# New orders of the instructions on all five queues of a pre-norm attention and GLU block

## The chip, the cores and the metric

One core of one Trainium2 chip runs the kernel. The metric is device time in microseconds (us) of one execution; a comparison is one of medians of such times. Below, PE is the matrix engine, DVE the vector engine, ACT the activation engine, POOL the general engine, and SP a queue that only issues transfers (DMAs); ACT issues a few too.

## The reference

Two blocks on 2048 tokens of width 448: linear attention with 16 heads of 28, then a gated feed-forward layer of width 1792, each behind a layernorm and with a residual.

```python
def _A_ref(x, wqkv, wo):
    qkv = (x @ wqkv).reshape(B, S, 3, H, Dh) ...
    phi = lambda t: jnp.where(t > 0, t + 1, jnp.exp(t)) + 1e-6
    pq, pk = phi(q), phi(k)
    kv = jnp.einsum("bhsd,bhse->bhde", pk, v)
    z = jnp.einsum("bhsd->bhd", pk)
    num = jnp.einsum("bhqd,bhde->bhqe", pq, kv)
    den = jnp.einsum("bhqd,bhd->bhq", pq, z)[..., None] + 1e-6
    return (num / den) ... @ wo
def _B_ref(x, w_gate, w_up, w_down):
    return (_gelu(x @ w_gate) * (x @ w_up)) @ w_down
h = x + _A_ref(_layernorm(x), A_wqkv, A_wo)
h2 = h + _B_ref(_layernorm(h), B_w_gate, B_w_up, B_w_down)
```

## The kernel before

The tokens are 16 tiles of 128 (numbers 0 to 15). V is never formed: the kernel sums phi(k) with the normalised input over all tokens, applies the V weights once, folds in wo, and gets the attention output from phi(q) normalised by its denominator.

**A graph and an order written out.** Every operation is a numbered task with a name; `_Graph.add` records what it reads and writes and from that its dependencies. `ORDERS` holds five strings, for PE, ACT, DVE, POOL and SP: the numbers of the tasks in the order in which each engine executes them. `place` takes them as they are, `plan` works out which semaphores each task waits for (a wait that another wait implies is dropped), and `emit` writes the instructions. An engine takes its tasks strictly in that order, so a task whose wait is not over holds back all that stand behind it. `HOLD` says which of several waits of a task is issued first.

**Stage 1, first layernorm and K, Q.** For tile t: `bnst1_t` and `bnag1_t` (DVE, lines 440 and 441) give the statistics, `ln1_t` and `rstd1_t` (ACT, 447 and 449) the reciprocal deviation, `negm1_t` (POOL, 444) minus the mean, and `normD_t` (DVE) or `normP_t`, `normT_t` (POOL, 507 and 510) the normalised tile. From tile 8 on, ln and rstd take two tiles at once. Tiles 0 to 3 are transposed on PE (`tr_t`) and copied out by `evxA_t` and `evxD_t`; the later ones by DMA transposes on SP (`xT_4` to `xT_14`, line 514; from tile 8 on two tiles each). `K2K3a`, `K2K3b` and so on are the projections of two tiles, in two halves, `K0`, `Q0`, `K1`, `Q1` those of one (536, 555). `ekN_t`, `ckN_t`, `pkN_t` (ACT, DVE, DVE; N tiles from t) make phi(k); `eqN_t` and `rqN_t` (ACT, 598 and 599) start phi(q). `pt10_t`, `pt30_t` and their like (PE, 590) are the sums over tokens.

**Stage 2.** `evp...`, `z0`, `z1` copy the sums out; `kv`, `kvm`, `w2a`, `w2b`, `evwA_g`, `evwD_g` form the product of the sums with the V and output weights, and eight small DMAs `dw2_0` to `dw2_7` repack it. For each pair of tiles p: `cq`, `aq` (DVE), `t1p` (POOL, 682), `dr`, `deA`, `rd`, `pn` (DVE, ACT) normalise phi(q); `pd` is a small copy on POOL; `oT_p` transposes by DMA (719); `outa_p`, `outb_p` are the output projection (751) and `hr` adds the residual. Pair 0 goes over PE transposes and copies (`tro`, `evoA`, `evoD`, `out1`). Then the second layernorm: `bnst2`, `bnag2`, `ln2`, `rstd2` (tiles 0 and 1) or `vpe2`, `pow2` (POOL, later tiles), `nhD` or `nhP`, `wrap`, and the transposes `trh` (PE, tiles 0 and 1) or `hT_t` (DMA, 807).

**Stage 3, feed-forward.** `guN_v` is block v of gate and up matmuls for N tiles (874 and 876, alternating between the two halves of the PE rows); `ge` is the gelu on ACT (898), `hm` the product on DVE (900). Tiles go in chunks of 2, 2, 4, 4 and 4: blocks 0 to 6, 7 to 13, 14 to 27, 28 to 41 and 42 to 55. `downa_t`, `downb_t` are the down projection of tiles t and t + 1 (825), `fo896_t` adds the residual (830) and `do_t` writes the output (814, 832). The last two tiles go one by one (843, 847). Gate and up of blocks share the PSUM banks 0, 1, 6 and 7, the down and the output projections 2, 3 and 4, 5.

**Transfers.** SP loads x, the K and Q weights, then issues the transposes, `dwv`, `dwv_t`, `dwo`, `dwg0` (gate weights) and `dwd_0` to `dwd_3` (down weights); ACT issues `dwu0` (up weights). All plain loads of a queue are chained in the order of their making:

```python
def dma(q, out_ap, in_ap, w, name, r=(), behind=()):
    own = [t for t in behind if t.eng == q]
    far = [t for t in behind if t.eng != q]
    t_ = G.add(q, lambda e: e.dma_start(out_ap, in_ap), r=r, w=w, name=name, kind="dma", after=own + last[q], sync=far)
    last[q] = [t_]
```

`after` only binds the order on the same queue; `sync` is a wait.

Of the kernel before, what the change touches and what calls it, by code (L numbers as in the profile page):

```python
# [12 lines left out]


ORDERS = (
# [29 lines left out]
)  # L45
HOLD = {
# [11 lines left out]
}  # L58

# [169 lines left out]
def bass_sequential_preLN__linear_attn_block__glu_gated_geglu__prompt_kernel(  # L229
    nc, A_x, A_wqkv, A_wo, B_x, B_w_gate, B_w_up, B_w_down, out  # L230
):
    S, D, FF, H, DH = 2048, 448, 1792, 16, 28
# [14 lines left out]
    WVQ = "sp"  # L247
# [14 lines left out]
    with es:  # L262
        block = es.enter_context(nc.Block())

        def sb(name, shape, dt):
            return es.enter_context(nc.sbuf_tensor(name, shape, dt))
# [6 lines left out]
        wv_sb = sb("wv_sb", [128, 4, D], BF16)  # L273
# [43 lines left out]
        def bufs(name, n):  # L317
            return [_Buf("%s%d" % (name, i)) for i in range(n)]
# [5 lines left out]
        b_w, b_wv = {"Q": bufs("wq", 3), "K": bufs("wk", 3)}, bufs("wv", 2)  # L324
# [18 lines left out]
        A_, B_ = slice(0, 64), slice(64, 128)  # L343
# [19 lines left out]
            return t_  # L363
# [4 lines left out]
        def rows3(src, c0, c1):  # L368
            return src[0:384, c0:c1].rearrange("(k p) n -> p k n", p=128)
# [240 lines left out]
            proj2(what)  # L610

        xts = [t for t in G.all if t.name.startswith("xT_")]
        dma(WVQ, wv_sb[:, 0:3, :], rows3(A_wqkv, 2 * D, 3 * D), [b_wv[0]], "dwv", behind=xts[3:4])
        dma(WVQ, wv_sb[A_, 3, :], A_wqkv[384:448, 2 * D:3 * D], [b_wv[1]], "dwv_t", behind=xts[3:4])
        dma(WVQ, wo_sb[:, :, :], A_wo.rearrange("(g p) n -> p g n", p=GW), [b_wo], "dwo", behind=xts[3:4])
        dma("sp", wgu_sb[A_, :, :], B_w_gate.rearrange("(k p) n -> p k n", p=64), b_wg, "dwg0", behind=xts[-1:])
        dma("act", wgu_sb[B_, :, :], B_w_up.rearrange("(k p) n -> p k n", p=64), b_wu, "dwu0", behind=xts[-1:])
# [355 lines left out]
```

## Time and profile before

| | before |
|---|---|
| three runs | 193.38, 193.20, 192.89 us, median 193.20 |
| the profiled execution | 193.26 us, its span 191.3 us |
| granted PE clock | 1.000 |
| busy in the span | PE 184.7, weight loads 101.3, DVE 125.3, ACT 71.4, POOL 52.4 us |
| DMA | 17.59 MB, mean 92 GB/s |

The span goes from the first to the last instruction that the profile shows; the execution is 2.0 us longer. Busy time is that of an engine's instructions, without waits; ends of matmuls are modelled, so PE looks a little busier than it is. A row of the timeline has the start from the span's beginning, the length, the engine and line, what is written and read, the shapes, and in brackets the idle time before it with what ended it. The chain that ended last is the sequence of work and waits that leads back from the last instruction.

### The profile page before, as it was taken

What the parts mean: (1) busy time and instruction counts of PE and PEld (TensorE: products, weight loads), DVE (VectorE), ACT (ScalarE), POOL (GpSimd) and SP (SyncE); (2) the same over time, 40 slices, a digit from 0 to 9 for tenths busy, and PEclk for the clock granted to TensorE, in tenths of its full rate; (3) what the DMA queues carried; (4) which work ended last, traced back from release to release, by engine and by line L of the source; (5) the groups of instructions that cost most, each with busy time, mean ns of one, the idle gap of its engine ahead of it and who ended that gap; (6) DMA issues with size and microseconds to landing.
All of it is one profiled execution on the core that took longest, in us unless ns stands there. A gap on an engine that the chain in (4) does not pass through costs nothing.

```text
span 191.3 us, 4741 instructions
## 1 busy us (share of the span) xinstructions
PE 184.7 (97%) x2010; PEld 101.3 (53%) x2010; DVE 125.3 (65%) x260; ACT 71.4 (37%) x164; POOL 52.4 (27%) x102
## 2 busy tenths in 40 slices
PE   7999899999799999999999999999999999999995
PEld 7544355554587667864444444454444444455443
DVE  2999748899999989996576837453444233444304
ACT  3686333699773203222223231232422213144100
POOL 5268910253045476701314420610000000000000
DMA  5933679995279623393302091000039000130002
GB/s 174 335 97 82 116 118 245 259 279 108 76 160 220 143 48 58 70 162 66 58 2 55 3 171 25 0 0 3 0 88 155 0 0 3 71 121 3 0 0 99
DMA packets 34244, 17.59 MB, mean 92 GB/s; under 512 B 27312, under 2 KB 32944, under 8 KB 34224
## 3 DMA queue, kind: packets, MB, share of 16 engines
q1 hardware_dynamic: 33472, 15.34, 36.8%
q10 hardware_dynamic: 752, 1.95, 3.8%
q8 instruction: 16, 0.26, 0.6%
q14 instruction: 4, 0.03, 0.1%
HBM read 8.37 MB, written 1.84 MB: 53 GB/s over the span
## 4 chain that ended last, share of the span: by engine, by line
PE 75%; DMA 11%; DVE 9%; SPq 2%; issue 0%; ACT 0%; POOL 0%
PE ps L874 30%; PE ps L825 18%; PE ps L876 7%; PE ps L555 6%; PE ps L590 4%; PE ps L751 4%; DVE st L440 3%; DMA hnT<-hn 3%; DMA pqnT<-pqn 3%; DMA x_sb<-in_A_x_dram 3%; PE ps L843 3%; DMA hh<-xnn 2%; SPq L361 1%; PE ps L736 1%; DVE pk L575 1%; SPq L807 1%
## 5 line engine op out<-in xcount | busy, mean ns | idle before, releaser
L874 PE MATMUL ps<-hnT,wgu_sb 64*128 64x512 bf16 (+1 forms) x490 | 88.7, 333 | 0.4 <-DMA hnT<-hn 0.4
L876 PE MATMUL ps<-hnT,wgu_sb 64*128 64x512 bf16 (+1 forms) x490 | 88.6, 333 | 0.0
L898 ACT ACTIVATE gl<-ps 128x256 bf16<-128x256 f32 (+1 forms) x84 | 35.0, 453 | 87.9 <-PE ps L874 86.7
L900 DVE TENSOR_TENSOR hh<-ps,gl 128x256 bf16<-128x256 f32 (+1 forms) x84 | 40.2, 507 | 38.4 <-ACT gl L898 38.1
L874 PEld LDWEIGHTS ps<-hnT,wgu_sb 64*128 64x128 bf16 x490 | 45.8, 94 | 34.1 <-DMA hnT<-hn 1.2
L876 PEld LDWEIGHTS ps<-hnT,wgu_sb 64*128 64x128 bf16 x490 | 45.8, 94 | 2.7
L825 PE MATMUL ps<-wd_sb,hh 64*128 64x448 bf16 x392 | 39.4, 349 | 0.0
L825 PEld LDWEIGHTS ps<-wd_sb,hh 64*128 64x128 bf16 x392 | 19.0, 94 | 18.6 <-issue 0.4
L555 PE MATMUL ps<-wqk_sb,hh 64*128 64x448 bf16 x196 | 23.4, 350 | 0.5 <-DMA hh<-xnn 0.3
L682 POOL TENSOR_TENSOR t<-pq,zbc 128x448 f32<-128x448 bf16 x15 | 16.0, 1084 | 24.9 <-DVE zbc L619 12.5
L440 DVE BATCH_NORM_STATS2 st<-x_sb 128x6 f32<-128x448 bf16 x32 | 19.1, 612 | 3.6 <-DMA x_sb<-in_A_x_dram 3.3
L830 DVE TENSOR_TENSOR x_sb<-ps,x_sb 128x896 bf16<-128x896 f32 x7 | 7.6, 1090 | 12.8 <-PE ps L825 12.8
L590 PE MATMUL ps<-pk,xnn 64*128 64x448 bf16 x128 | 15.2, 350 | 0.5 <-DVE pk L575 0.4
L555 PEld LDWEIGHTS ps<-wqk_sb,hh 64*128 64x128 bf16 x196 | 9.0, 94 | 10.4 <-PE ps L555 1.5
L572 ACT ACTIVATE e<-ps 128x896 bf16<-128x896 f32 (+1 forms) x10 | 7.5, 760 | 7.4 <-PE ps L555 7.4
L751 PE MATMUL ps<-w2p,pqnT 64*128 64x448 bf16 x84 | 9.9, 349 | 0.4 <-DMA pqnT<-pqn 0.4
L774 POOL TENSOR_SCALAR hn<-x_sb,nm,rs 128x448 bf16<-128x448 bf16 x14 | 9.9, 714 | 0.4
L590 PEld LDWEIGHTS ps<-pk,xnn 64*128 64x128 bf16 x128 | 6.1, 94 | 7.2 <-DVE pk L575 2.0
L686 DVE TENSOR_REDUCE den<-t 128x32 f32<-128x896 f32 (+1 forms) x9 | 8.8, 973 | 1.7 <-POOL t L682 1.6
L575 DVE SCALAR_TENSOR_TENSOR pk<-ps,e 128x896 bf16<-128x896 f32 (+1 forms) x10 | 9.0, 904 | 0.2
L758 DVE TENSOR_TENSOR x_sb<-ps,x_sb 128x896 bf16<-128x896 f32 (+1 forms) x9 | 8.8, 978 | 0.1
L507 POOL TENSOR_SCALAR xnn<-x_sb,nm,rs 128x448 bf16<-128x448 bf16 (+1 forms) x12 | 8.3, 695 | 2.0 <-ACT rs L449 1.7
(85 smaller groups left out, 138.4 us busy)
## 6 DMA issues: line engine op xcount, KB each, us to landing
wgu_sb<-in_B_w_gate_dram SPq DMA_DIRECT2D x1, 1568.0 KB, 14.6
wgu_sb<-in_B_w_up_dram ACTq DMA_DIRECT2D x1, 1568.0 KB, 16.5
out_dram<-x_sb SPq DMA_DIRECT2D x7, 224.0 KB, 2.3
x_sb<-in_A_x_dram SPq DMA_DIRECT2D x3, 448.0 KB, 6.1
wd_sb<-in_B_w_down_dram SPq DMA_DIRECT2D x2, 448.0 KB, 5.0
wqk_sb<-in_A_wqkv_dram SPq DMA_DIRECT2D x2, 336.0 KB, 4.9
wd_sb<-in_B_w_down_dram SPq DMA_DIRECT2D x2, 336.0 KB, 6.3
wo_sb<-in_A_wo_dram SPq DMA_DIRECT2D x1, 392.0 KB, 5.9
```

The costliest lines, as they stand in the source:

```text
L440: op("dve", lambda e: e.bn_stats(st[:, t, :], src_ap), [b_src], [b_st[t]], "bnst%s_%d" % (tag, t))
L555: ins = e.matmul(ps[:, bk0 + i_, 0:D], xnT[HALF[h], t, c, :], wqk_sb[HALF[h], c, c0:c0 + D], start=(part == "a" and c == 0), stop=(c == 3))
L575: op("dve", lambda e: e.scalar_tensor_tensor(pk[:, ip:ip + n, :], psK, EPS, e1[:, i:i + n, :], ALU.max, ALU.add), b_ps[bu:bu + n] + b_e1[i ...
L590: ins = e.matmul(ps[:, BK_PT[c], 0:D], xnn[HALF[h], t // 2, tcols(t, c)], pk[HALF[h], t % PK_R, :], start=(t == 0 and o == 0), stop=(t == ...
L682: op(eng, lambda e, t=t, n=n: e.tensor_tensor(t1[:, n, :], pq[:, t, :], zbc[:, :], ALU.mult), [b_pq[t]] + b_z, [b_t1[n]], "t1%s_%d" % (eng ...
L751: ins = e.matmul(ps[:, BK_OUT[n], 0:D], pqnT[rows, i2, n, g, :], w[rows, g, :], start=(g == 0 and s == 0), stop=(g == 3 and s == 1))
L774: op("pool", lambda e, t=t, sh=sh: e.tensor_scalar(hn[:, sh, 0:D], x_sb[:, t, :], nm2[:, t:t + 1], rs2[:, t:t + 1], ALU.add, ALU.mult), [b ...
L825: ins = e.matmul(ps[:, BK_O[n], 0:D], hh[HALF[h], j, (t % HR) * 128:(t % HR + 1) * 128], wd_sb[HALF[h], j, :], start=(s == 0 and j == 0), ...
L874: first = e.matmul(psG[:, jj * N:(jj + 1) * N], wgu_sb[A_, k, j * 128:(j + 1) * 128], hnT[A_, r0:r0 + nt, ka_, :], start=(k == 0), stop=(k ...
L876: ins = e.matmul(psU[:, jj * N:(jj + 1) * N], wgu_sb[B_, k, j * 128:(j + 1) * 128], hnT[B_, r0:r0 + nt, kb_, :], start=(k == 0), stop=(k = ...
L898: G.add("act", lambda e, gi=gi, cs_=cs_, psG=psG: e.activation(gl[:, gi, cs_], psG[:, cs_], AF.Gelu_apprx_tanh), r=[b_ps[BK_G[i]]], w=b_gl ...
L900: op("dve", lambda e, dst=dst, srcU=srcU, srcL=srcL: e.tensor_tensor(dst, srcU, srcL, ALU.mult), [b_ps[bu]] + b_glh, [b_ar[j_][t % HR] for ...
```

## The change

The five orders are new, and with them `HOLD`. The same tasks are executed, none is added or removed. In the last hunk the loads of the V weights no longer name the fourth transpose as something that they stand behind.

What moves, by name:

- SP: `xT_7` before `xT_6`; `dw2_0` to `dw2_3` before `oT_1`; `dwd_1` to `dwd_3` before `oT_2`; `oT_7` before `oT_6`; `hT_8` before `hT_10`; `do_0` from before `oT_5` to behind `hT_10`; `do_4` before `hT_14`; `do_6` from before `hT_14` to behind `do_12`, near the end; `do_12` and `do_6` before `do_14`.
- ACT: `evxA_0` before `ln1_1`; `ln1_4` and `rstd1_4` before `evxA_3` and `eq1_1`; `ln1_7` and `rstd1_7` before `ln1_6`; `dwu0` behind `ek1_15` and `ek1_14`; `rq2_4` before `z1`; `evwA_0` before `deA2_2` and `evoA_0`; `eq2_10` before `evoA_1`; many exchanges of neighbours.
- DVE: `bnag1_1` behind `evxD_0`; `bnst1_5` before `evxD_3`; the statistics of tiles 14 and 15 behind `pk2_4`; `ptpad` and `wvpad` to the front; `aq_4` before `evpD_3`; `cq_6` before `evwD_1`; `pn1_1` and `pn2_2` later; `aq_10`, `dr2_14`, `wrap2_8`, `wrap2_10` earlier; `fo896_2` 14 places later, `fo896_6` 14 earlier and `fo896_10` 14 later; many exchanges.
- POOL: `eps` before `ones`; `mones`, `mask_a`, `mask_b` to the front; `mhalf` and `powwarm` from the front to between the `t1p`; `normP_7`, `normT_7` before `normP_6`; `t1p_10` before `nhP_3`; `pd_14` before `vpe2_8` and `pd_12`.
- PE: `K1` before `Q1`; `pt30_4` and several other sums behind the next projection; `Q10Q11a` before `w2a`; `outa_5`, `outb_5` three places earlier, `downb_2` six later; even blocks before odd ones through most of chunks 2 and 3; `downa_6` two and `downb_6` six places earlier; `downa_10` two and `downb_10` five later.

The diff, cut where `HOLD` and the context are long (task numbers used here: 255, 256 `dwv`; 323, 361 `oT_1`, `oT_2`; 324 to 331 `dw2_0` to `dw2_7`; 332 to 335 `dwd_0` to `dwd_3`; 571, 595 `hT_12`, `hT_14`; 424, 543, 547 `do_0`, `do_4`, `do_6`; 98, 99 `ln1_4`, `rstd1_4`; 259 `dwu0`):

```diff
@@ -13,47 +13,46 @@
 
 
 ORDERS = (
-    "27 33 757 61 41 65 49 80 58 68 83 84 72 76 77 92 78 73 79 93 74 90 111 112 75 88 91 135 89 136 118 116 155 119"
-    " 117 156 140 175 142 141 176 143 160 195 162 196 161 215 180 216 181 163 182 231 200 232 201 223 183 224 202 225"
-    " 226 203 227 228 235 229 230 236 239 266 240 269 268 243 270 271 244 247 288 248 291 294 295 251 252 311 307 336"
-    " 400 337 403 406 409 412 362 418 415 363 421 386 422 449 387 452 455 435 458 461 436 464 467 470 498 501 471 507"
-    " 504 484 513 510 485 519 516 558 525 559 522 531 582 528 583 537 534 540 601 596 541 606 611 616 544 621 626 631"
-    " 636 641 545 651 646 661 656 666 679 674 667 689 684 670 699 671 694 709 704 719 714 729 724 739 734 744 748 745"
+    "27 33 757 61 41 65 49 68 58 80 83 84 76 72 77 92 73 93 78 79 74 75 111 88 112 90 89 135 91 136 118 155 116 156"
+    " 117 119 175 140 176 142 141 195 143 160 196 162 161 215 163 216 180 231 181 232 200 182 201 183 223 224 202 225"
+    " 226 203 227 228 235 229 230 236 239 266 240 243 268 269 270 271 244 247 288 248 291 294 295 251 252 311 307 336"
+    " 400 337 403 406 409 412 362 418 415 363 421 386 422 449 387 452 455 435 458 461 436 464 467 470 498 501 484 504"
+    " 507 485 510 513 471 516 519 558 522 525 559 528 531 582 534 537 583 540 596 601 541 611 544 606 545 616 621 626"
+    " 631 636 641 646 651 656 661 666 674 679 667 689 684 699 694 670 709 704 719 714 671 729 724 739 734 744 748 745"
     " 751 754",
-    "1 3 26 30 31 38 39 34 46 54 47 62 42 55 66 50 67 81 59 98 99 69 105 82 106 122 85 129 123 130 148 149 95 94 168"
-    " 169 113 188 208 189 209 137 157 177 197 259 220 217 233 260 263 234 264 237 281 285 238 241 242 320 274 245 289"
-    " 272 292 246 249 250 304 305 302 303 312 308 254 357 253 314 401 404 407 381 413 410 419 416 430 450 453 479 456"
-    " 459 462 465 468 553 499 502 508 577 505 514 511 520 517 526 523 532 529 538 535 602 604 597 599 607 609 614 612"
-    " 619 617 622 624 629 627 632 634 637 639 644 642 654 652 647 649 662 664 659 657 680 682 677 675 690 687 685 692"
-    " 702 700 697 695 712 710 707 705 722 720 717 715 732 730 727 725 740 742 737 735",
-    "28 29 36 32 37 44 35 52 45 40 53 25 48 43 63 64 96 51 97 60 127 103 128 104 120 70 121 71 144 146 86 147 87 145"
-    " 206 166 164 207 165 186 167 187 184 185 204 114 205 115 138 139 158 159 178 179 315 198 199 316 221 222 218 276"
-    " 219 277 24 352 262 261 278 280 265 284 282 286 267 283 319 287 273 275 321 290 322 293 353 296 297 300 301 298"
-    " 299 310 306 376 313 474 309 356 377 358 359 338 425 339 402 380 426 341 405 408 340 382 342 383 411 414 429 420"
-    " 347 417 364 350 365 548 475 572 367 366 431 368 432 423 478 451 549 388 454 389 457 391 392 390 374 480 460 552"
-    " 463 398 437 466 481 469 440 573 438 554 500 439 555 503 441 576 509 472 506 578 515 579 512 486 487 521 488 489"
-    " 490 518 527 560 447 524 563 561 564 496 533 562 530 539 536 584 587 585 586 603 605 600 588 598 542 608 610 613"
-    " 594 618 615 570 620 623 625 630 628 633 635 638 640 645 643 546 655 653 648 650 663 665 660 658 683 678 676 681"
-    " 668 688 691 686 693 703 701 672 698 696 713 711 708 706 723 721 718 716 733 731 728 726 741 743 738 736 746 749"
+    "1 3 26 30 31 34 38 46 39 47 62 42 54 55 66 50 67 98 99 59 69 105 106 129 81 82 130 85 122 148 123 149 94 95 168"
+    " 169 113 188 189 137 208 209 157 177 197 220 217 259 233 234 260 263 264 281 237 285 238 242 241 274 272 320 289"
+    " 245 292 246 250 249 304 305 302 303 312 308 254 357 253 314 401 404 407 381 410 413 419 430 416 450 453 456 459"
+    " 479 553 462 465 468 577 499 502 505 508 511 514 517 520 523 526 529 532 535 538 599 597 604 602 614 607 612 609"
+    " 617 619 622 624 627 629 634 632 637 639 644 642 649 647 652 654 657 659 662 664 675 677 682 680 692 690 687 685"
+    " 700 695 702 697 712 710 705 707 722 720 717 715 732 730 725 727 740 742 735 737",
+    "25 28 29 36 32 44 35 45 37 52 40 48 53 24 63 43 64 96 51 97 103 60 104 127 70 128 144 71 120 145 146 121 147 86"
+    " 87 164 166 167 165 184 186 187 185 114 115 206 204 207 205 138 139 158 159 315 178 179 276 198 199 277 218 219"
+    " 316 221 222 352 353 262 261 278 280 265 284 286 282 267 283 319 376 273 275 287 290 321 293 322 296 297 300 301"
+    " 298 299 310 474 306 313 377 309 356 425 358 359 475 338 402 341 426 380 342 339 405 408 382 383 340 411 414 429"
+    " 420 431 347 417 364 350 367 548 365 368 549 366 432 478 423 451 388 389 454 391 572 392 390 374 457 552 460 398"
+    " 573 463 480 437 466 481 469 576 578 440 554 555 500 441 503 579 506 509 438 486 487 439 515 512 489 488 490 518"
+    " 447 521 496 472 524 527 560 530 561 533 536 563 564 584 539 587 588 598 603 605 542 562 585 586 600 613 608 610"
+    " 615 546 618 620 623 625 628 630 594 570 635 633 638 640 645 643 650 648 653 655 658 660 665 663 678 676 681 683"
+    " 668 693 691 688 686 701 696 703 698 713 711 706 708 716 718 723 721 733 731 726 728 672 741 743 738 736 746 749"
     " 752 755",
-    "10 23 12 17 16 14 15 11 18 56 57 19 100 101 131 107 108 109 20 13 124 125 133 132 150 152 153 151 170 172 190 21"
-    " 171 173 191 192 193 210 212 213 22 211 279 317 318 355 354 360 378 379 428 427 384 343 344 345 346 349 476 370"
-    " 433 477 369 371 551 550 373 372 394 393 395 397 396 482 556 574 575 442 580 443 444 492 491 445 493 494 495 446"
-    " 566 565 567 590 568 591 589 592 593 569",
-    "0 2 4 5 6 7 8 9 102 110 126 134 154 174 194 214 255 256 257 258 323 324 325 326 327 328 329 330 331 332 361 333"
-    " 334 335 385 348 351 434 375 399 424 483 557 581 497 448 547 595 571 673 543 473 669 750 747 753 756",
+    "12 10 16 20 21 17 11 56 19 57 22 18 100 101 107 109 131 108 132 133 124 150 125 152 151 153 170 172 173 190 13 23"
+    " 171 191 192 193 210 211 212 213 279 317 318 354 14 355 360 378 379 15 427 428 343 344 384 345 346 476 349 477"
+    " 369 370 433 550 371 551 373 372 393 394 395 396 397 574 575 482 580 443 444 556 442 445 446 492 491 493 495 494"
+    " 590 591 589 565 566 567 593 568 569 592",
+    "0 2 4 5 6 7 8 9 102 110 134 126 154 174 194 214 255 256 257 258 324 325 326 327 323 328 329 330 331 332 333 334"
+    " 335 361 385 348 351 434 375 399 483 581 557 448 497 424 543 595 571 673 473 669 747 547 750 753 756",
 )
 HOLD = {
...
     755: (754,),
 }
 
@@ -610,8 +609,8 @@
             proj2(what)
 
         xts = [t for t in G.all if t.name.startswith("xT_")]
-        dma(WVQ, wv_sb[:, 0:3, :], rows3(A_wqkv, 2 * D, 3 * D), [b_wv[0]], "dwv", behind=xts[3:4])
-        dma(WVQ, wv_sb[A_, 3, :], A_wqkv[384:448, 2 * D:3 * D], [b_wv[1]], "dwv_t", behind=xts[3:4])
+        dma(WVQ, wv_sb[:, 0:3, :], rows3(A_wqkv, 2 * D, 3 * D), [b_wv[0]], "dwv")
+        dma(WVQ, wv_sb[A_, 3, :], A_wqkv[384:448, 2 * D:3 * D], [b_wv[1]], "dwv_t")
         dma(WVQ, wo_sb[:, :, :], A_wo.rearrange("(g p) n -> p g n", p=GW), [b_wo], "dwo", behind=xts[3:4])
         dma("sp", wgu_sb[A_, :, :], B_w_gate.rearrange("(k p) n -> p k n", p=64), b_wg, "dwg0", behind=xts[-1:])
         dma("act", wgu_sb[B_, :, :], B_w_up.rearrange("(k p) n -> p k n", p=64), b_wu, "dwu0", behind=xts[-1:])
```

19 rows, old and new, of the table HOLD are left out of this document.

## The prediction

> **What bounds the kernel now.** The page comes first, for the span and the bound.
>
> ```profile
> span 191.3 us, 4741 instructions
> PE 184.7 (97%) x2010; PEld 101.3 (53%) x2010; DVE 125.3 (65%) x260; ACT 71.4 (37%) x164; POOL 52.4 (27%) x102
> q8 instruction: 16, 0.26, 0.6%
> ```
>
> TensorE (PE) is busy for 97% of the span and the change leaves its work alone. New orders can only win back PE's idle time, so the second view is the busy time by stage (columns: stretch, length, then busy time and instructions of PE, weight loads, DVE, ACT, POOL; clock, DMA share, GB/s).
>
> ```profile
> 5.00:16.00 11.00, 10.49 (x104) 4.94 (x103) 10.56 (x33) 7.79 (x28) 5.87 (x16) 1.00 0.63 193
> 16.00:22.10 6.10, 5.33 (x52) 2.22 (x53) 5.37 (x14) 4.59 (x11) 5.58 (x13) 1.00 0.44 91
> 22.10:46.60 24.50, 24.45 (x264) 12.82 (x266) 19.74 (x38) 14.65 (x24) 6.55 (x11) 1.00 0.86 198
> 46.60:51.20 4.60, 3.38 (x56) 1.64 (x57) 4.14 (x12) 3.38 (x9) 1.51 (x2) 1.00 0.56 128
> 51.20:64.70 13.50, 13.15 (x223) 11.06 (x222) 13.37 (x22) 7.41 (x13) 7.20 (x11) 1.00 0.83 169
> 64.70:140.00 75.30, 75.30 (x832) 40.67 (x830) 51.57 (x99) 19.98 (x46) 23.16 (x40) 1.00 0.26 49
> 140.00:150.00 10.00, 9.62 (x94) 4.58 (x92) 3.90 (x9) 2.63 (x8) 0.00 (x0) 1.00 0.74 116
> 150.00:189.00 39.00, 39.00 (x370) 19.57 (x365) 14.78 (x33) 9.21 (x28) 0.00 (x0) 1.00 0.07 27
> ```
>
> PE idles 0.51 before 16, 0.77 to 22.1, 0.05 to 46.6, 1.22 to 51.2, 0.35 to 64.7, 0.38 in 140 to 150, and nothing elsewhere: 3.28 us in all. That is too little by the overlap of matmuls, which two neighbours in the timeline show:
>
> ```profile
> 140.01 0.38 PE L874 MATMUL ps<-hnT,wgu_sb 64*128 64x512 bf16 x1
> 140.23 0.38 PE L874 MATMUL ps<-hnT,wgu_sb 64*128 64x512 bf16 x1
> ```
>
> Each is drawn 0.38 long and the next starts after 0.22, so a stall loses 0.16 more than the idle drawn. What ends the stalls stands in the chain that ended last (start, length, what):
>
> ```profile
> 17.98 4.06 DMA hh<-xnn
> 22.08 0.74 PE ps L555 x6
> ...
> 54.31 5.94 DMA pqnT<-pqn
> 60.29 0.74 PE ps L751 x6
> ...
> 139.79 1.10 DVE x_sb L830
> 140.91 0.35 SPq L832
> 141.30 1.43 SPq L807
> 142.77 6.00 DMA hnT<-hn
> ...
> 148.81 0.39 PE ps L874
> ```
>
> Three transposes end a PE stall the moment they land: xT_8 (K8K9a at 22.08), oT_2 (outa_2 at 60.29) and hT_12 (the first gate and up block of the last tiles at 148.81). The stall at 46.6 to 51.2 is the second layernorm of tiles 0 and 1, a chain over DVE and ACT.
>
> **The change part by part.**
>
> **1. hT_12 (a gain of 0.5).** In the rows above the SP queue holds hT_14 and hT_12 behind do_6, the output of tiles 6 and 7, which waits for an addition that ends at 140.89. The new SP order has do_0 and do_4 there instead, and do_6 fourth from the end. do_4 waits for fo896_4 behind downb_4, which is eight gate and up blocks of 1.5 and a half of a down block earlier, some 15 us; the wraps that feed the two transposes come on DVE behind block 34, four blocks before the one at 140, so near 136. Even with 6.00 to land hT_12 is there by about 144, and its reader stands at 148.3 without the stall. The stall goes whole: 0.38 drawn plus 0.16, 0.54. What is late next in 140 to 150: nothing, PE has no other wait there. Bounds 0.4 to 0.55.
>
> **2. The start (a gain of 0.7).** POOL's normalisations feed the transposes, and its chain starts on ACT:
>
> ```profile
> 9.46 0.55 ACT L599 ACTIVATE pq<-ps 128x448 bf16<-128x448 f32 x1
> 9.85 0.17 DVE L441 BATCH_NORM_AGGREGATE mv<-st 128x2 f32<-128x6 f32 x1
> 10.57 0.33 ACT L447 ACTIVATE ln<-mv,eps_t 128x1 f32<-128x1 f32 x1
> 10.93 0.20 ACT L449 ACTIVATE rs<-ln 128x1 f32<-128x1 f32 x1
> 11.23 0.71 POOL L507 TENSOR_SCALAR xnn<-x_sb,nm,rs 128x448 bf16<-128x448 bf16 x1 [0.91 <-ACT rs L449]
> 19.68 1.09 DVE L575 SCALAR_TENSOR_TENSOR pk<-ps,e 128x896 bf16<-128x896 f32 x1
> 20.83 0.93 PE L590 MATMUL ps<-pk,xnn 64*128 64x448 bf16 x8 [0.38 <-DVE pk L575]
> ```
>
> Tile 4's statistics are there at 10.02, yet ACT takes ln1_4 only at 10.57, behind eq1_1 and evxA_3. The new order puts ln1_4 and rstd1_4 ahead of both: ln1_4 at 10.05, normP_4 at about 10.65, 0.58 earlier. POOL is nearly full from there to normP_8, so xT_8 is issued near 17.3 instead of 17.98. On DVE the statistics of tiles 14 and 15 move behind pk2_4 (the row at 19.68), which brings it forward by about 0.7 and with it pt10_4, the stall at 20.83.
>
> There are costs in front: bnag1_1 moves behind evxD_0, so normD_1 and tr_1 come some 0.4 later, and evxD_3 behind bnst1_5 holds K2K3 another 0.4. PE waits for xT_4 and xT_5 after that anyway, so they are covered; if POOL were not the limit they would cost 0.4. Laid end to end, PE is free for K8K9a near 20.5. How long the landing then takes is the open size:
>
> ```profile
> DMA to landing us min/median/max: 2.4/2.8/4.1
> ...
> DMA to landing us min/median/max: 3.0/3.1/5.9
> ```
>
> The first row is the xT transposes (half of them single tiles), the second the oT ones, all of two tiles. A two-tile transpose takes 3.1, xT_8 took 4.06. Undisturbed it lands at 20.4, K8K9a starts 1.6 earlier, and as pt30_4 (four matmuls of 0.19, 0.38) now comes behind it, the stage gains 1.2. If whatever held xT_8 for 1.0 now holds xT_8 or xT_10, 0.2 is left. I take the middle, 0.7: of these transposes the median is undisturbed, but this stage had one that was not.
>
> **3. oT_2 and the down weights (a loss of 0.2).** Old order: dwd_0, oT_2, dwd_1 to dwd_3. New: all four dwd, then oT_2. Also dw2_0 to dw2_3 now stand ahead of oT_1.
>
> ```profile
> 52.78 0.59 SPq L361 DMA_DIRECT2D wd_sb<-in_B_w_down_dram  x1
> 54.31 1.26 SPq L719 DMA_TRANSPOSE pqnT<-pqn  x1
> 55.61 1.79 SPq L361 DMA_DIRECT2D wd_sb<-in_B_w_down_dram  x3
> ...
> 58.00:59.50 1.50, 1.50 (x32) 1.33 (x30) 1.50 (x4) 0.01 (x1) 1.24 (x2) 1.00 0.04 5
> 59.50:60.50 1.00, 0.65 (x14) 0.27 (x10) 1.00 (x5) 0.53 (x2) 0.80 (x1) 1.00 1.07 317
> ```
>
> SP idles from 53.37 to 54.31, waiting for pd_4, so the issues of dwd fit in before. Their bytes (14 blocks of 112 KB, 1568 KB) take 5.0 us at the 317 GB/s of the last row. If they flow from 52 they are through near 57, and oT_2 lands at 58 to 59, ahead of its reader: the stall (0.35 drawn in this stage) goes, 0.5 gained. If they flow only from 54 and the hole of 1.5 falls among them, oT_2 lands near 62.4, a loss of 2.1. I take 0.2, as the queue moves oT_2 back by about as much as the earlier issues move it forward. oT_1 comes about 1 later on its queue and has the layernorm stall as cover; without that it would cost its lateness.
>
> The row at 58 is a hole: 5 GB/s, with transfers queued on both sides of it. One rule of the Trainium skill speaks to it. Runtime: NRT & Kernel Launch, section Instruction fetch mechanics, says that the crossing of a 16 KiB block of code costs one bump of a queue's tail and is mostly hidden. By it no transpose would be held by a code load, part 2 would give its 1.2 and the sum would be 0.5 lower, towards the first rival. The trace speaks against it for DMA if the hole is one of the 16 code loads of q8; no view used here gives their times.
>
> Another speaks against this move. DMA: Bandwidth & Descriptors, section Queues, rings and completion order, has descriptors consumed in ring order on each engine. By it oT_2 cannot pass the down weights, which is the third rival; a queue that let it pass would give the 0.5.
>
> **4. The layernorm stall, 46.6 to 51.2 (nothing).** PE's order is the same. On DVE cq_6 takes the place of aq_4, but pn2_2 now stands ahead of hr1_0. evwA_0 is no longer late for out1_0, yet evoA_1 and evoD_1 then end the wait. 0, bounds -0.2 and +0.3.
>
> **5. The rest (a loss of 0.05, bounds 0 to 0.4).** PE exchanges of gate and up blocks and of down blocks: no idle is drawn from 64.7 to 140, and each exchange keeps its slack. The tightest is downa_6, one block after downb_4: the addition fo896_4 takes 1.10, one block 7 times 0.22, 1.5. oT_7 ahead of oT_6 makes SP wait for outb_5, but outb_5 moves forward too; outa_6 comes about 1 us after oT_6 lands. dwu0 is issued about 2 us later:
>
> ```profile
> wgu_sb<-in_B_w_up_dram ACTq DMA_DIRECT2D x1, 1568.0 KB, 16.5
> 187.93 0.33 SPq L814 DMA_DIRECT2D out_dram<-x_sb  x1
> 188.31 0.43 SPq L832 DMA_DIRECT2D out_dram<-x_sb  x1
> 188.92 0.83 SPq L814 DMA_DIRECT2D out_dram<-x_sb  x2
> ```
>
> From about 31 it lands at 47.6, and gate and up begin near 50; beyond 2.4 of further delay each us counts. At the end do_12, do_6 and do_14 need 0.4 each from 187.4, done at 188.6 before the last two: covered. The dropped waits on dwv and dwv_t change nothing, as all DMAs of SP are chained. Constants on POOL move into its idle time.
>
> **Sum.** -0.54 - 0.7 + 0.2 + 0.05 and 0.1 for small waits at the block after downa_2 (hT_6 is issued earlier): -1.1. The profiled execution took 193.26 (span 191.3 and 2.0 around it), 0.06 over the median of 193.2. 193.26 - 1.1 = 192.2.
>
> **Rivals.** *All of it lands:* transposes undisturbed and oT_2 ahead of the hole, -0.54 - 1.2 - 0.5 and nothing lost: 191.0. The medians of 2.8 and 3.1 speak for it, 4.06, 5.94 and 6.00 against. *The start gives nothing:* xT_10 is held as xT_8 was, or the slip of tr_1 and K2K3 comes through; -0.54 and the two small losses leave about 192.8, within 0.3% (0.58 us) of 193.2, about what a measurement of this kernel can tell. For it: the stage had such a landing, and it has two waits that gain only together. *oT_2 queues behind the down weights and the hole:* its landing at 62.4 costs 2.1; with 0.54 and the part of the start that it leaves (0.7), 194.1. It decides from a landing after 62.1 on the old clock. Against it: dwd has some 2 us of earlier issue.
>
> **Numbers.** Forecast 0.53, own range 191.5 to 192.6; first rival 0.15, second 0.20, third 0.12. Faster 0.68, same 0.20, slower 0.12. The range goes from the first rival to half of the third: 190.9 to 193.7.
>
> **What would show it.** Right: no wait of gate and up on hnT near 148; K8K9a at 20.5 to 21.5; PE idle before 22 below 1.0. Wrong: outa_2 waiting more than 0.5 for pqnT, K10K11a waiting for hh, or new PE waits on ACT or DVE in 64 to 180.

## The result and the profile after

The changed kernel takes 194.61 us in the median, the kernel before 192.89 in the same comparison: a ratio of 1.0061, 95% interval 1.0035 to 1.0087 (the ratio leaves out five executions more than 1.5% over the shortest). It is 0.6% slower, where 192.2 and faster was forecast.

The profiled execution of the changed kernel does not show that. It took 192.99 us, less than the 193.26 of before. The page's first lines, then the answer on the cores, and then the same answer for another profiled execution of the same kernel (called e1 below):

```profile
span 190.9 us, 4736 instructions
PE 183.8 (96%) x2010; PEld 102.1 (53%) x2010; DVE 125.0 (66%) x260; ACT 72.4 (38%) x164; POOL 53.3 (28%) x102
```

```profile
core 0: 190.9 us, clock 1.000
```

```profile
core 0: 192.3 us, clock 0.991
```

The last column is the mean clock that TensorE was granted. Of the 20 executions, 16 have a mean clock of 0.982 or 0.991 and take 194.4 to 196.8; the other four have 0.999 or 1.000 and take 192.27, 192.99, 193.12 and 193.76. In three later sets of the kernel before, 81 executions together, four had 0.991. So there are two questions: what the change does at full clock (their median of 193.05 is level with before), and why it loses the full clock.

The busy time by stage of the profiled execution, with the columns of the table in the prediction:

```profile
5.00:16.00 11.00, 9.91 (x101) 4.40 (x100) 10.09 (x32) 8.60 (x28) 6.52 (x17) 1.00 0.65 193
16.00:22.10 6.10, 5.76 (x58) 2.86 (x58) 5.09 (x13) 3.76 (x8) 5.93 (x13) 1.00 0.51 107
46.60:51.20 4.60, 2.31 (x46) 1.07 (x44) 4.48 (x12) 3.46 (x9) 0.00 (x0) 1.00 0.65 130
51.20:64.70 13.50, 13.40 (x224) 11.80 (x226) 13.09 (x23) 7.31 (x13) 8.12 (x12) 1.00 0.70 166
140.00:150.00 10.00, 10.00 (x100) 4.96 (x98) 3.78 (x10) 3.24 (x10) 0.00 (x0) 1.00 0.29 54
```

PE has no idle left in 140 to 150 (9.62 of 10 before) and more work in 16 to 22 (5.76, before 5.33), but less in 5 to 16 (9.91, before 10.49). In 46.6 to 51.2 it works only 2.31, before 3.38. The timeline of PE tells why, here with the SP queue's (changed kernel), and below them, from the kernel before, oT_1's issue, the last projections and the same output projection:

```profile
46.20 1.74 PE L554 MATMUL ps<-wqk_sb,hh 64*128 64x448 bf16 x14
48.99 0.35 PE L790 MATMUL ps<-ident,hn 64*128 64x64 bf16 x12 [1.05 <-DVE hn L770]
49.70 0.35 PE L790 MATMUL ps<-ident,hn 64*128 64x64 bf16 x12 [0.21 <-DVE hn L770]
51.16 0.93 PE L750 MATMUL ps<-w,pqnT 64*128 64x448 bf16 x8 [0.96 <-DMA pqnT<-pqn]
```

```profile
43.39 2.63 SPq L360 DMA_DIRECT2D w2p<-w  x4
46.07 1.44 SPq L718 DMA_TRANSPOSE pqnT<-pqn  x1
```

```profile
45.28 1.26 SPq L719 DMA_TRANSPOSE pqnT<-pqn  x1
```

```profile
46.53 1.74 PE L555 MATMUL ps<-wqk_sb,hh 64*128 64x448 bf16 x14
50.36 1.09 PE L751 MATMUL ps<-w,pqnT 64*128 64x448 bf16 x8
```

outa_1 now waits 0.96 for oT_1. That transpose is issued at 46.07, behind dw2_0 to dw2_3, 0.79 later than before. It lands at 51.02, before at 48.42: 4.95 us after its issue instead of 3.14. From 47.9 to 51.2 PE has nothing but two small groups of transposes.

### The profile page after: what moved, and what is told of

The parts are those of the page before. It is cut to its first block, busy times and chain, and to the rows that moved or that the text cites. A ratio compares the mean times of both kernels' runs of the same rounds, so it can differ in the third digit from the quotient of the medians.

```text
span 190.9 us, 4736 instructions
## 1 busy us (share of the span) xinstructions
PE 183.8 (96%) x2010; PEld 102.1 (53%) x2010; DVE 125.0 (66%) x260; ACT 72.4 (38%) x164; POOL 53.3 (28%) x102
## 4 chain that ended last, share of the span: by engine, by line
PE 86%; DMA 6%; DVE 3%; ACT 1%; POOL 1%; issue 0%; ACTq 0%; POOLq 0%
PE ps L873 43%; PE ps L824 19%; PE ps L554 8%; PE ps L589 6%; PE ps L750 5%; PE ps L842 3%; DMA pqnT<-pqn 3%; DMA x_sb<-in_A_x_dram 2%; PE ps L875 2%; DMA hh<-xnn 1%; POOL xnn L506 1%; DVE st L439 1%; DVE pqn L690 1%; PE ps L630 1%; ACT ln L446 1%
## 5 line engine op out<-in xcount | busy, mean ns | idle before, releaser
L451 POOL TENSOR_SCALAR ln<-mv 128x2 f32<-128x2 f32 x7 | 1.5, 219 | 27.0 <-DVE mv L440 26.6
```

## Experiments

Every ratio is to the kernel before, run beside it on the same chip; "mean clock below 1" counts executions of 0.982 to 0.991. The theories: T1, the idle of PE around 48 to 51 costs the clock; T2, the start does; T3, the chip was slower that time.

**e1, the changed kernel unaltered.**

> The changed kernel unaltered, to see the clock. Theory T1 (the late oT_1 leaves PE so idle around 48 to 51 us that the clock is halved for a stretch): in most executions the mean granted clock is 0.991 and the time 194.4 to 194.9; a profile with that mean shows one stretch of 3.4 us at half clock that begins between 49 and 54 us. Rival T2 (the idle time at the start does it): the same mean, but the stretch begins between 7 and 16 us. Rival T3 (the chip was merely slower then): clock 1.000 and about 193.0.

194.74 us against 192.99, ratio 1.0069 (1.0042 to 1.0096); 11 of 12 executions with a mean clock below 1. The stretches around the pit (columns as above, the clock is the third number from the end):

```profile
44.58:48.00 3.42, 2.82 (x21) 0.93 (x19) 3.32 (x7) 3.01 (x6) 0.00 (x0) 1.00 1.04 183
48.00:51.41 3.41, 1.48 (x38) 1.04 (x40) 3.39 (x9) 2.49 (x7) 0.00 (x0) 1.00 0.51 117
51.41:54.82 3.41, 3.41 (x34) 2.66 (x31) 2.17 (x4) 2.34 (x3) 1.58 (x3) 0.50 0.96 307
```

Right behind the pit, and nowhere else from 7.04 us (where the full clock begins) to the end, the clock is 0.50 for 3.41 us, which loses 1.7 us of work. T1 has the place; T2 and T3 fall.

**e2, the kernel before with oT_1 made late** (dw2_0 to dw2_3 ahead of it, and dwu0 late).

```diff
-(SP)  ... 258 323 324 325 326 327 328 ...
+(SP)  ... 258 324 325 326 327 323 328 ...
-(ACT) ... 259 220 217 ...
+(ACT) ... 220 217 259 ...
```

> The kernel before, with two parts of the change alone: dw2_0 to dw2_3 issued ahead of oT_1 on SP, and dwu0 issued behind ek1_15 and ek1_14 on ACT. T1: oT_1 lands 1.5 us or more later than its 48.4, outa_1 waits about 0.5 to 1.5 us, and the granted clock falls below 1.000 in most executions: 194 to 196 us. T2: the wait appears, but the clock stays 1.000 and the time is 193.4 to 194.4. T3: as T2.

194.94 us, ratio 1.0092 (1.0067 to 1.0118); five of six with a clock below 1. Two successive stretches, with the columns as above:

```profile
47.92:51.33 3.41, 1.92 (x44) 1.03 (x42) 3.03 (x11) 2.25 (x7) 0.34 (x1) 1.00 0.63 138
51.33:54.74 3.41, 3.41 (x32) 2.61 (x30) 2.76 (x4) 3.05 (x4) 0.56 (x2) 0.50 0.34 66
```

These two edits alone bring the slowdown. Here oT_1 is late by its issue (47.63): it took 3.1 us.

**e3, the changed kernel with the two edits undone.**

```diff
-(SP)  ... 258 324 325 326 327 323 328 ...
+(SP)  ... 258 323 324 325 326 327 328 ...
-(ACT) ... 220 217 259 ...
+(ACT) ... 259 220 217 ...
```

> The changed kernel with those two parts taken back: oT_1 ahead of dw2_0, dwu0 ahead of ek1_15. T1: the wait of outa_1 (1.0 us) goes and the clock is 1.000 in nearly all executions: 191.7 to 192.4 us. T2: the wait goes, the clock stays at 0.991 in most: 193.4 to 194.0. T3: 192.0 with the clock at 1.000 here and in the changed kernel alike.

196.50 us, ratio 1.0153 (1.0113 to 1.0193), all six below full clock: a miss. oT_1, issued at 46.11, still took 4.9 us and held outa_1 to 51.16; and the wait moved on to oT_2:

```profile
DMA to landing us min/median/max: 4.9/4.9/4.9
```

```profile
52.95 2.23 SPq L360 DMA_DIRECT2D wd_sb<-in_B_w_down_dram  x4
55.22 8.29 SPq L718 DMA_TRANSPOSE pqnT<-pqn  x2
```

```profile
62.97 0.76 PE L750 MATMUL ps<-w2p,pqnT 64*128 64x448 bf16 x6 [2.47 <-DMA pqnT<-pqn]
```

```profile
60.15:63.56 3.41, 0.94 (x15) 0.39 (x12) 3.38 (x6) 0.60 (x1) 1.98 (x6) 1.00 0.34 49
63.57:66.98 3.41, 3.41 (x36) 2.47 (x34) 0.03 (x1) 0.23 (x1) 2.88 (x4) 0.50 0.38 72
```

With dw2 behind oT_1 the four dwd are issued up to 55.2, and oT_2 behind them lands at 62.92, after dwd_3 (62.18). The clock falls behind this pit instead. (e9 below is e3 with oT_2 ahead of dwd_1 to dwd_3 again, and takes 193.16.) Why oT_1 still took 4.9 us with dwu0 already landed (46.34) was open: theory A, for which e9 and e10 were made.

**e4, the changed kernel with 18 matmuls that nobody reads ahead of outa_1.**

```diff
+        def keep(e):
...
+            for _ in range(18):
+                ins = e.matmul(ps[:, 0, 0:128], ones_bf[:], ones_bf[:], start=True, stop=True)
+            return ins
...
-(PE)  ... 307 336 ...
+(PE)  ... 307 758 336 ...
```

> The changed kernel with 18 more matmuls of 128 columns on PE ahead of outa_1, whose product nobody reads: they fill the wait of 1.0 us and save no work. T1: clock 1.000 in most executions, time 192.8 to 193.3, faster than the changed kernel by about 1.6 us though PE does more. T2: no change, 194.4 to 194.9. T3: no change.

193.46 us, ratio 1.0017 (0.9995 to 1.0040), none of 12 below full clock. oT_1 took 5.4 us in its profiled execution, so the wait is still there:

```profile
49.32 1.18 PE L924 MATMUL ps<-ones_bf 128*128 128x128 bf16 x18
50.73 0.93 PE L750 MATMUL ps<-w,pqnT 64*128 64x448 bf16 x8 [0.22 <-DMA pqnT<-pqn]
```

More work for PE makes the kernel 1.3 us faster than e1, beside it. That is the clock's part, taken out by PE's activity alone.

**e5, the kernel before with do_6 behind hT_12.**

```diff
-(SP)  ... 448 547 595 571 673 ...
+(SP)  ... 448 595 571 547 673 ...
```

> The kernel before, with one edit: on SP the two sixths-group output transfers do_6 go behind hT_12 (before: ahead of hT_14). If the wait for hT_12 near 148 was on the path, it goes (0.54 us at the gate and up matmul behind downa_8) and nothing takes its place: 192.4 to 192.6 us where the kernel before has 193.0, ratio 0.997 to 0.998. If the time is given back behind it (do_6 late at the end, or the next gate and up matmul waits instead), 193.0, ratio 1.000. The granted clock stays at 1.000 in both.

192.47 us, ratio 0.9974 (0.9962 to 0.9985): 0.5 us, as expected. The wait at 148 is gone and nothing takes its place: the down block runs into the next gate and up block.

```profile
145.50 2.81 PE L825 MATMUL ps<-wd_sb,hh 64*128 64x448 bf16 x28
148.14 0.38 PE L874 MATMUL ps<-hnT,wgu_sb 64*128 64x512 bf16 x1
```

**e6 and e7, the two edits of e2 one by one.** e6 has SP's, e7 ACT's.

> The kernel before, with one edit: on SP dw2_0 to dw2_3 go ahead of oT_1; dwu0 stays early. If SP's order alone makes oT_1 late: oT_1 is issued near 47.6 (before 45.3), lands near 50.8, outa_1 starts near 50.9 with about 0.4 us of waiting, TensorE is granted half its clock from about 51.3 for 3.4 us, and the time is about 194.9 us, ratio 1.009. If dwu0's lateness is needed too: oT_1 lands before 50.0, the clock stays 1.000, and the time is within 0.3 us of the kernel before, ratio 0.999 to 1.002.

> The kernel before, with one edit: on ACT the transfer dwu0 is issued behind ek1_14 (some 2 us later); SP's order stays. If the up weights still flowing make oT_1 slow by themselves: oT_1, issued at 45.3, takes about 5 us instead of 3.1, lands past 50, and half the clock follows, about 194.5 us, ratio 1.007. If only SP's order matters: oT_1 lands before 49.7, the clock stays at 1.000, and the time is within 0.3 us of the kernel before.

e6: 193.17 us, ratio 1.0020 (0.9991 to 1.0048), four of 12 below full clock (194.0 to 194.7), the others 192.4 to 193.6. oT_1 is issued at 47.55 and lands at 50.68, 3.1 later; outa_1 starts at 50.81. The mechanism came as expected in the profiled execution, itself one of the four, but in a third of the executions instead of in most, so the time is that of the other expectation. e7: 193.41, ratio 1.0021 (1.0003 to 1.0040), none below full clock. oT_1, issued at 45.46 while dwu0 flows (it lands at 48.57), took longer, but not 5 us:

```profile
DMA to landing us min/median/max: 4.1/4.1/4.1
```

It landed at 49.59, still under the layernorm. Alone, neither edit costs more than some 0.2%; together, in e2, they cost 0.9% and the clock in five of six executions.

**e8, the changed kernel with the old orders of all engines between 24 and 75 us**: the tasks that both kernels start in that stretch keep their places, in the old sequence; SP's part is the one of e9 below.

> The changed kernel, with the orders of all engines between 24 and 75 us put back as in the kernel before (the work that both kernels start in that stretch, in the old order on the places it holds); the start and the part behind 75 us stay changed. If the whole loss sits in the middle stretch: oT_1 lands near 48.4, the clock stays at 1.000, the start's 0.2 us and the 0.5 to 0.7 us behind 75 us are left as a gain: 192.2 to 192.5 us, ratio 0.995 to 0.998. If the start or the end of the change costs something, or its code loads meet the transposes again, 193.0 us or more, ratio 1.000 and above.

193.86 us, ratio 1.0036 (1.0008 to 1.0063), five of 12 below full clock: not the expected gain. oT_1 is as before (issued at 45.27, landed at 48.38), but the seam at 75 us made a wait that neither kernel has:

```profile
80.79 0.28 PE L875 MATMUL ps<-hnT,wgu_sb 64*128 64x256 bf16 x1 [1.32 <-DVE hh L899]
```

With the 0.16 of overlap the mixed orders cost some 1.5 us of their own there, so this run says nothing of the start. Its clock was useful (below).

**e9 and e10, why oT_1 takes 5 us.** e9 puts SP's old order and the early dwu0 back into the changed kernel; e10 also PE's old order from 24 to 56 us.

```diff
 e9:
-(SP)  ... 258 324 325 326 327 323 328 329 330 331 332 333 334 335 361 ...
+(SP)  ... 258 323 324 325 326 327 328 329 330 331 332 361 333 334 335 ...
-(ACT) ... 220 217 259 ...
+(ACT) ... 259 220 217 ...
 e10 besides:
-(PE)  ... 119 175 140 176 142 141 195 143 160 196 162 161 215 163 216 180 ... 240 243 268 269 ...
+(PE)  ... 119 175 140 142 141 176 143 160 195 162 196 161 215 180 216 181 ... 240 269 268 243 ...
```

> The changed kernel, with SP's order between 38 and 64 us as in the kernel before (oT_1 ahead of dw2_0 to dw2_3, oT_2 ahead of dwd_1) and dwu0 early again on ACT; TensorE, DVE, ACT and POOL stay changed. Theory A, the 16 KB code load of TensorE, which falls at 49.0 us in the changed order and at 50.3 in the old one, holds up oT_1's end: issued at 45.4 to 46.1, oT_1 lands near 51.0 although nothing else is in flight, TensorE waits 0.9 us before outa_1, and the clock is halved for 3.4 us in more than half of the executions: 194.0 to 194.8 us, ratio 1.005 to 1.010. Theory B, only the weights around it made oT_1 slow: it lands 3.1 us behind its issue, by 49.3; the clock stays; 192.6 us, ratio 0.997 to 0.999.

> The same, with TensorE's order between 24 and 56 us put back too (nine neighbours exchanged; the code load should fall near 50.3 again). Theory A: oT_1 lands 3.1 us behind its issue, by 49.3, TensorE does not wait before outa_1, most executions keep the full clock: 192.4 to 192.9 us, ratio 0.996 to 1.000. Theory B: no difference to the run without TensorE's order put back.

e9: 193.16 us, ratio 1.0004 (0.9976 to 1.0032), four of 12 below full clock. e10: 192.10, ratio 0.9956 (0.9934 to 0.9977), two of 12, less than expected. The landing of oT_1 in e9, then in e10:

```profile
DMA to landing us min/median/max: 4.8/4.8/4.8
```

```profile
DMA to landing us min/median/max: 3.1/3.1/3.1
```

q8 is a queue of code loads, 16 KB each. That they are TensorE's is inferred: e9 and e10 differ in PE's order alone, and the load that matters here starts when 464 matmuls have started in e9, and 498 in e10. Its row in the stretch from 50.7 to 51.9 of e9, between issue (48.14) and landing (52.90) of oT_1, and from 49.6 to 51.0 of e10, behind the landing (48.65):

```profile
q8 instruction: 1, 0.02, 4.6%
```

```profile
q8 instruction: 1, 0.02, 5.2%
```

The packets put the load at 50.82 in e9 and at 49.76 in e10. It fell inside oT_1's transfer in every run in which oT_1 took 4.8 to 5.4 us (the changed kernel, e1, e3, e4, e9), and behind the landing in those with 3.1 (before, e2, e5, e8, e10, e11, e12; in e6 0.1 ahead of it). Theory A has the transfer right. It expected too much time for e9: the wait before outa_1 was 0.70 (the profile names ACT's second copy of hnT, which ends at 52.92 beside oT_1's landing, but before, outa_1 starts at 50.36, ahead of that copy at 50.48) and the clock fell in a third of the executions. (The profiled execution of e9 was its longest, 194.84, with a start some 2 us late though its mean clock is 1.000. Its records of the full clock begin only at 10.46: four matmuls of line 535 take 1.76 at 6.96, where the changed kernel has 1.02 at 6.73. The mean does not show such a late start. This trace is read for oT_1 only.)

**e11, the kernel before with e5's edit and the changed start**: on all engines the tasks that both kernels start before 24 us take the changed sequence.

```diff
-(ACT) ... 67 81 59 98 99 69 ...
+(ACT) ... 67 98 99 59 69 105 106 129 81 82 ...
-(SP)  ... 102 110 126 134 154 ... 448 547 595 571 ...
+(SP)  ... 102 110 134 126 154 ... 448 595 571 547 ...
...
```

> The kernel before with do_6 behind hT_12 (0.9974 alone), and the changed kernel's orders on all engines for the work that starts before 24 us. If the start of the change is worth what its traces show (kv 0.2 us earlier): 192.3 us, ratio 0.996 to 0.997. If the start gives nothing: 192.5, 0.9974. If it costs: 192.8 or more.

191.45 us, ratio 0.9920 (0.9900 to 0.9939), all six at full clock: better than all expectations, and the best version here, 0.8% below the kernel before. Its stages up to 22 us, and K8K9a in PE's timeline:

```profile
5.00:16.00 11.00, 10.17 (x103) 4.50 (x104) 10.27 (x31) 8.92 (x29) 7.16 (x17) 1.00 0.67 196
16.00:22.10 6.10, 5.99 (x61) 3.12 (x63) 5.33 (x16) 3.68 (x9) 5.63 (x14) 1.00 0.62 118
```

```profile
20.48 0.55 PE L590 MATMUL ps<-pk,xnn 64*128 64x448 bf16 x4
20.87 0.73 PE L555 MATMUL ps<-wqk_sb,hh 64*128 64x448 bf16 x6
```

**e12, the same with eight idle matmuls ahead of trh_1.**

```diff
+                    if t == 1:
+                        def keep(e, banks=banks):
...
+                            for _ in range(8):
+                                ins = e.matmul(ps[:, banks[0], 0:128], ones_bf[:], ones_bf[:], start=True, stop=True)
+                            return ins
+                        G.add("pe", keep, r=[b_ones], w=[b_ps[banks[0]]], name="keep")
```

> The same, with eight more matmuls of ones (128x128 by 128 columns, nothing reads them) on TensorE ahead of the transposes trh_1, in 0.9 us that it idles. In traces so far the clock is halved only behind a stretch of 3.41 us in which fewer than about 3,250 columns, weighted by the share of 128 rows in use, went through TensorE; the lowest stretch of the kernel before holds 2,816, so 8 x 128 more lift it to 3,840 and no execution should show half a clock around 50 us. Time as without them, within 0.2 us. If the extra work delays the transposes instead, 0.3 to 0.9 us more.

191.88 us, ratio 0.9943 (0.9923 to 0.9964), all six at full clock. That is 0.4 over e11, where 0.2 at most was expected, but the intervals of the two overlap. e11 was at full clock without them, so they bought nothing that can be seen in six executions.

## Why the prediction was wrong, step by step

**1, hT_12: right.** Forecast 0.5 (0.4 to 0.55), measured by e5 alone: 0.26% of 193.0, 0.5.

**2, the start: within its bounds, but less in the changed kernel than in e11.** Forecast 0.7 with bounds 0.2 and 1.2. e11 against e5 (0.9920 and 0.9974) is 0.54%, 1.0 us. There K8K9a starts at 20.87, within the 20.5 to 21.5 named, and xT_8 and xT_10 land 3.2 and 3.1 us after their issues: undisturbed, the upper bound's case. In the changed kernel's own profile PE idles 1.43 before 22, not less than 1.0 as named, K8K9a comes at 21.51, and 0.33 is left at the last projections (46.20, before 46.53): xT_5 to xT_8 were issued 0.7 later than in e11. In e1, the same kernel, 0.8 is left there.

What held xT_8 before can be read, though no run tests it. In the five profiles with the old start (before, e2, e5, e6, e7) it takes 4.0 to 4.1, and an 8 KB load of q14, another queue of instruction loads, starts some 1.6 us ahead of its landing. In the nine with the changed start it takes 3.1 to 3.2, and that load starts 0.2 ahead of the landing or later. Its row in the kernel before, 20.3 to 20.8:

```profile
q14 instruction: 1, 0.01, 3.9%
```

**3, oT_1: the step that failed.** It said "oT_1 comes about 1 later on its queue and has the layernorm stall as cover; without that it would cost its lateness." The first half was right (0.79 at issue). But oT_1 also took 1.8 longer to land, as a code load fell into it: 4.8 in e9, where dwu0 has landed before its issue, and 3.1 in e10, which differs from e9 in PE's order alone. dwu0's bytes can lengthen it too (e7: 4.1), but are not needed: in e3 dwu0 landed 0.2 behind oT_1's issue, and oT_1 still took 4.9. Together it is 2.6 later; the cover was 1.6, the wait 0.96. The step put that at nothing, and took the duration of a moved transfer from where it used to be.

The rest of step 3 was about oT_2. It landed at 60.12 (before 60.24), and PE, later by then, no longer waited for it, so neither the loss nor the third rival came: PE idles 0.10 in 51.2 to 64.7, 0.35 before. But e3 shows the rival's mechanism, once dw2 no longer goes ahead of oT_1: oT_2 behind the down weights, 2.47 of waiting. The ring order of the section Queues, rings and completion order in DMA: Bandwidth & Descriptors of the Trainium skill agrees with that: oT_2 landed after all four dwd. The same section says that completion is not first in, first out for an issuing engine, so the prediction's "cannot pass" is more than it states.

The hole that the prediction asked about goes with a code load: one of q8 starts at 57.80 in the kernel before, inside oT_2's 5.94 us, and one at 145.97, inside hT_12's 6.00. The row of the first, from 57.7 to 59.5:

```profile
q8 instruction: 1, 0.02, 3.2%
```

**4 and 5: right.** The wait before trh_1 is 1.05 where 0.94 stood. dwu0 landed at 47.83 (47.6 forecast); nothing on PE waited for it. Of the signs named for a wrong prediction none appeared.

**What no step had: the clock.** The trace's records of it are on a grid of 3.41 us; in e1 the full clock begins at 7.04 and the half at 51.41, 13 such windows later. The grid's place in the kernel changes from execution to execution. In the table each matmul counts its columns times the share of the 128 rows that it uses, by its start.

| run | window from | PE drawn busy | columns weighted | clock of the next window |
|---|---|---|---|---|
| e3 | 60.15 | 0.94 | 1,856 | 0.5 |
| e1 | 48.00 | 1.48 | 2,200 | 0.5 |
| e2 | 47.92 | 1.92 | 2,648 | 0.5 |
| e6 | 47.77 | 1.96 | 2,704 | 0.5 |
| e8 | 47.08 | 2.19 | 3,040 | 0.5 |
| e3 | 46.50 | 2.08 | 3,008 to 3,456 (two matmuls start at its edge) | 1.0 |
| e7 | 48.27 | 2.26 | 3,488 | 1.0 |
| changed | 49.17 | 2.24 | 3,872 | 1.0 |
| changed | 45.76 | 2.29 | 3,912 | 1.0 |

In the profiled execution of the changed kernel the grid split the pit between two windows, and the clock held:

```profile
45.76:49.17 3.41, 2.29 (x29) 0.77 (x27) 3.31 (x9) 2.77 (x7) 0.00 (x0) 1.00 1.01 198
49.17:52.58 3.41, 2.24 (x53) 1.64 (x47) 3.27 (x9) 2.71 (x6) 0.00 (x0) 1.00 0.27 62
```

With a limit of 3,250, an estimate, each trace gives the share of grid positions that have a window below it. Below it stand the executions below full clock:

| | before | changed | e1 | e2 | e3 | e4 | e5 | e6 | e7 | e8 | e9 | e10 | e11 | e12 |
|---|---|---|---|---|---|---|---|---|---|---|---|---|---|---|
| share | .17 | .71 | all | .59 | all | .25 | .16 | .59 | .17 | .57 | .64 | .31 | .17 | 0 |
| executions | 4 of 81 | 16 of 20 | 11 of 12 | 5 of 6 | 6 of 6 | 0 of 12 | 0 of 12 | 4 of 12 | 0 of 12 | 5 of 12 | 4 of 12 | 2 of 12 | 0 of 6 | 0 of 6 |

The order is nearly the same, but the shares are not exact, as one profiled execution stands for all. The low ones are too high: at .16 to .25, before, e4, e5, e7 and e11 together would give some 22 of 123 executions (an estimate), and four fell; with a limit of 3,040 the same traces give .02 to .06. Nor does the count serve at the kernel's start: in e9 the full clock begins behind a window of 3,104, and not behind the one of 3,136 ahead of it.

TensorE: Matmul & The Clock Gate of the Trainium skill, section Part 1: The HAM clock gate, describes a free-running window of 3413 ns with half clock after an idle one, and the traces agree on the window and the half clock; but here the window before the half clock held up to 2.19 us of drawn matmul time, and in e1, e2, e6 and e8 no idle gap in it was longer than 1.2 us.

**The account.** Where PE stands in the two profiled executions, both at full clock (start of each in us):

| | before | changed | difference |
|---|---|---|---|
| last projections | 46.53 | 46.20 | -0.33 |
| first gate and up matmul | 51.17 | 51.91 | +0.74 |
| first down projection | 64.68 | 64.98 | +0.30 |
| last down projections | 177.92 | 177.54 | -0.38 |

The start gave 0.33. The pit took 1.07: 0.96 is the wait for oT_1 and 0.1 the longer layernorm. Then 0.44 came back where oT_2's stall had stood (the sum had a loss of 0.2 there), and 0.68 behind that, of which 0.5 is hT_12. The two spans, 190.9 and 191.3, differ by the same 0.4. Half a clock for 3.41 us then costs another 1.5 in four of five executions (193.05 is the median of the four at full clock, 194.6 that of the eleven at 0.991 up to 195.0).

## What to carry to other kernels

A transfer that is moved on its queue must be priced at its new place: what bytes and which code loads are in flight there, not what it took before. A stall that "covers" a late input is also a stall that gets longer, and an engine kept half idle over a whole clock window pays again behind it; where the pit can't be closed, work that nobody reads can be cheaper than the clock (e4). And one profiled execution may be of the rare kind: look at the clock of all executions before reading its trace as the result.

## What the runs showed of the hardware that was not expected

- In the nine windows of the table the clock is halved for 3.41 us behind 3,040 weighted columns or fewer and kept behind 3,488 or more; the one at 3,008 to 3,456 kept it. Drawn busy time does not separate them (2.19 halved, 2.08 kept).
- A code load, inferred to be TensorE's, lengthens a two-tile DMA transpose from 3.1 to 4.8 us and more. Runtime: NRT & Kernel Launch of the Trainium skill, section Instruction fetch mechanics, calls the fetch mostly hidden; for the engine itself no run speaks against it, for the DMAs e9 and e10 do.
- Where the load falls follows the engine's own order: with neighbours exchanged on PE, and 464 matmuls ahead of 48 us in both kernels, it starts at 50.27 before and at 49.02 in the changed kernel; e9 and e10 differ in PE's order alone, and show it.
